# One attention half prepared earlier, weight splits ordered behind units, partial sums in score tiles, and chunk order 0, 2, 1

## The chip, the cores and the metric

The kernel runs on one core of one Trainium2 chip. The metric is the device time of one execution in microseconds (us). Engines are named as in the profile: PE (matmul), PEld (its weight loads), DVE (VectorE), ACT (ScalarE), POOL (GpSimd) and SP, whose queue issues nearly all DMAs.

## What is computed

Three stages follow each other. Inputs q, k, v and alpha are [4, 8, 768, 48] (batch, heads, steps, head size).

```python
for t in range(S):
    state = alpha[:, :, t, :, None] * state + einsum(k[:, :, t], v[:, :, t])
    y[:, :, t] = einsum(q[:, :, t], state)
x = y.transpose(0, 2, 1, 3).reshape(3072, 384)

h = x @ w_in                       # 384 -> 2048
g = (a0 + a1*h + a2*h**2 + a3*h**3) / (1 + |b0|*|h| + |b1|*h**2 + 1e-6)
x = g @ w_out                      # 2048 -> 384

h = x @ w2_in                      # 384 -> 1024
solu = h * softmax(h)
out = (layernorm(solu) * g_ln) @ w2_out
```

## The kernel before

Steps are cut into six chunks of 128 (times four batches: 512 tokens a chunk). Every product is computed with operands split into a high and a low part (three matmuls for one: hi*hi, hi*lo, lo*hi).

**First stage, by halves.** A chunk's attention is done in two halves of two batches, so there are 12 halves, numbered 0 to 11; the "fourth half" is index 3, the "fifth" index 4. `a_prep(i)` prepares a half: DVE transposes alpha, k and q (L294, L299), runs two scans over alpha (L312, L321), multiplies k by the second (L324) and transposes it back (L328); POOL multiplies q by the first (L339). The result goes to scratch memory (`kb_d`, `qk_d`) and is read back in another layout (`qks`, L280; `kns`, L286). `a_pe(i)` computes the half: scores (`sc`, L424), copied to tiles `A` by ACT (L431) and masked by POOL (L432), then `y` (L448), written as a high and a low part of the token tile `xt` (L474 on ACT, L475 on DVE), then the state update (`u`, L487). `qks`, `kns` and the scratch tiles of the preparation exist once.

**Second stage, by units.** A unit is one chunk and one block of 128 of the 2048 hidden columns; there are 96, numbered u = 0 to 95. `m_up(u)` is nine matmuls into one of three banks `h` (L604) and a chain of elementwise operations on ACT and DVE, with POOL in some units (L609 to L635); its last DVE operation, L628 or L635, is recorded as `fin[u]` and frees the bank. `gh` (ACT) and `gl` (POOL, L638) are the parts of the result. `m_down(u)` follows four units later: nine matmuls (L650) into three accumulation banks of the chunk. The order of units is written by hand: chunk 0 blocks 0 to 11 (u = 0 to 11), chunk 1 blocks 0 to 7 (u = 12 to 19), chunk 0 blocks 12 to 15, chunk 1 blocks 8 to 15, then chunks 2 to 5. So the sums of chunks 0 and 1 leave in two parts (`x2b_d` and `x2_d`; `x2e`, L657 to L660), which are added when the third stage loads them (`n_load`, L686 to L699).

**Weights.** Group n holds blocks 4n to 4n+3. `w1_group(n)` loads and splits it in seven steps (`split_w`: load to a staging tile `st` or a lent place, three DVE operations L541, L544 and L545, a copy on ACT and a difference on POOL). `w2_split` does the same for the third stage in 14 steps and writes the parts to scratch memory.

**Third stage.** Tiles of 128 tokens: `n_up`, softmax and norm, `n_turn`, `n_down`, `n_out`. The four tiles of the first chunk are put among the last units; the other tiles follow the last unit. `n_load` writes to the buffers of tag `xt`, of which there are two, so the second chunk's load waits for the last unit's up matmuls.

**What sets the order.** The loop over u (L895 on) calls, in this order: a weight step (`take(prep, 1)`; `CONV` says at which u a group begins), `m_up(u)`, a step of the half in work (`take(side, 1)`; `BEGIN` says at which u a half begins), a step of `w2_split` at u = 20, 31, 32, 39, 40 and so on, and `m_down(u - 4)`. A step of a half (`half_steps`) is one step of `a_pe(i)` and two of the preparation of half i+1; `LINGER = {3: 16}` makes the preparation of half 4 wait until u = 16, although half 3 begins at u = 8. The framework then orders each engine's instructions with a simulated timeline; the resulting queues are fixed. `tc.issue_after(x)` makes the instructions of a block on x's engine come behind x. `pin(n)` does that for a unit's last PE instruction at u and for ACT, POOL and `fin` at u - n; `later(n)` for `fin[u - n]` alone:

```python
def later(n):
    return tc.issue_after(fin[now[0] - n].ins) if n <= now[0] < GE + n and now[0] - n in fin else ExitStack()
```

Weight groups two and three are not pinned.

Of the kernel before, what the change touches and what calls it, by code (L numbers as in the profile page):

```python
# [30 lines left out]
def kernel(  # L31
# [21 lines left out]
    CH = 128  # L53
# [20 lines left out]
    PRE = (1, 1, 0, 0)  # L74
    GP = 2
    GS = 2
    G1 = 99
    G2 = 3
    MIX = lambda u: u < 24 and u % 2 == 0
    EARLY = (9, 11, 13, 15)  # L80
    SKIP = (5, 7, 11)
    AHEAD = 3
    U2, IDLE = 20, (0, NF1 // 2 - 1)
    BEGIN = {2: 2, 8: 3, 21: 4, 27: 5}
    BEGIN.update({16 * c + 2 + 8 * x: 2 * c + 2 + x for c in range(2, NCH - 1) for x in range(2)})
    CONV = {0: 2, 13: 3}
    LINGER = {3: 16}
    assert (B, H, D, CH) == (4, 8, 48, 128)

    const = ctx.enter_context(tc.tile_pool(name="const", bufs=1, side="left"))  # L90
# [66 lines left out]
    def network(fast):  # L157
# [257 lines left out]
        def a_pe(i):  # L415
# [4 lines left out]
            for p in range(2):  # L420
                sc = [ps_ap.tile([128, B, CH], F32, name="sc", tag="at") for j in range(2)]
                for x in range(B):
                    for j in range(2):
                        nc.tensor.matmul(  # L424
                            sc[j][:, x, :],
                            lhsT=hf.k[p][64 * j:64 * j + D, x, :], rhs=hf.q[p][64 * j:64 * j + D, x, :],
                            start=True, stop=True,
                        )
                for j in range(2):
                    t = A[p, j] = ap_.tile([128, B, CH], F32, name="A", tag=f"A{p}{j}")  # L430
                    nc.scalar.activation(t, sc[j], AF.Copy)  # L431
                    nc.gpsimd.affine_select(  # L432
                        out=t, in_=t, pattern=[[0, B], [1, CH]], compare_op=ALU.is_ge, fill=0.0, base=0,
                        channel_multiplier=-1,
                    )
                yield
# [204 lines left out]
        def m_down(u):  # L641
            c, f = order[u]
            n, o = divmod(f, 4)
            if (c, f) in first:
                x2ps[c] = [ps_x2p.tile([128, NTOK], F32, name=f"x2p{d}", tag=f"x2p{d}") for d in range(KT)]
            gh, gl = gts.pop(u)
            hi, lo = wo[n]
            for d in range(KT):
                for w, gg in ((hi, gh), (hi, gl), (lo, gh)):
                    nc.tensor.matmul(  # L650
                        x2ps[c][d], lhsT=w[:, o, 128 * d:128 * d + 128], rhs=gg,
                        start=((c, f) in first and w is hi and gg is gh), stop=((c, f) in final and w is lo),
                    )
            if (c, f) in final:
                to = x2_d[c] if f == NF1 - 1 else x2b_d[c]
                for d0, n in ((0, 2), (2, 1)):
                    e = moe_pool.tile([128, 2, NTOK], F32, name="x2e", tag="st", bufs=2)  # L657
                    for d in range(n):
                        nc.scalar.activation(e[:, d], x2ps[c][d0 + d], AF.Copy, scale=back if fast else 1.0)  # L659
                    nc.sync.dma_start(out=to[:, d0:d0 + n, :], in_=e[:, :n])  # L660
                del x2ps[c]
# [23 lines left out]

        def n_load(c):  # L686
            t = x2s[c] = moe_pool.tile([128, KT, 2, NTOK], F32R, name="x2", tag="xt", bufs=2)
            for kt in range(KT):
                raw = t[:, kt, 1].bitcast(F32)
                nc.sync.dma_start(out=raw, in_=x2_d[c][:, kt, :])  # L690
# [109 lines left out]

        def n_out(s, op):
            c, qq = divmod(s, 4)
            o = moe_pool.tile([128, DM], F32, name="o", tag="st", bufs=2)
            nc.scalar.activation(o, op, AF.Copy)
            to = out.rearrange("(b c q j) d -> c q b j d", b=B, c=NCH, q=4)[c, qq]
            for b in range(B):
                (nc.scalar if s == NCH * B - 1 and b >= 2 else nc.sync).dma_start(out=to[b], in_=o[32 * b:32 * b + 32])
# [64 lines left out]
        def half_steps(i):  # L872
            gp = a_pe(i)
            gd = chain(a_prep(i + 1), a_move_qk(i + 1) if i + 1 >= NPE else iter(()), a_load(i + 2, ("ra", "rk")) if i + 2 < NH and i + 1 >= NPE else iter(())) if i + 1 < NH else iter(())
            b = "wait"
            while True:
                with pin(GP):
                    a = next(gp, "end")
                if now[0] >= LINGER.get(i, 0):
                    with pin(GS):  # L880
                        b = next(gd, "end")
                        if b != "end":
                            b = next(gd, "end")
                if a == "end" and b == "end":
                    if i + 1 < NH:
                        _run(a_enter(i + 1))
                        if i + 2 < NH and i + 1 < NPE:
                            _run(a_load(i + 2))
                    return
                yield  # L890
# [5 lines left out]
        for u in range(NU + LAG):  # L896
# [5 lines left out]
            if u < NU:  # L902
# [7 lines left out]
                if fast and u in CONV:  # L910
                    _run(prep)
                    stage["near"] = CONV[u] == 2
                    prep = w1_group(CONV[u])
                take(prep, 1)
                m_up(u)
            if u == NU:
                _run(n_load(1))
            take(side, 1)
            if u == U2 or (u > U2 and u % (NF1 // 2) in IDLE and u not in (23, 24)):
                stage["bank"] = "at" if fast else ""  # L920
                with later(G2):
                    take(split2, 1)
# [150 lines left out]
```

## Time and profile before

| | us |
|---|---|
| median of 3 runs (794.39 to 795.79) | 794.52 |
| the profiled execution's own time | 793.51 |
| its span, first to last instruction | 791.8 |
| PE busy | 735.1 |
| DVE busy | 624.9 |
| ACT busy | 540.1 |
| POOL busy | 351.0 |

Shares of busy time are means over stages with different limits. Windows of the span, with the busy time of each engine in each, say more, and the timeline says at which instruction an engine stood and what released it. Units run from about 57 to 594 us, the third stage to the end.

### The profile page before, as it was taken

The page shows a single profiled execution, that of the slowest core. Times are in us where ns is not written, and L with a number is a line of the kernel's source. Part 1 is how long each engine was busy: PE and PEld are TensorE (multiplying, and loading weights), DVE is VectorE, ACT ScalarE, POOL GpSimd, SP SyncE. Part 2 cuts the span into 40 slices and gives each one's busy share as a digit, 9 for nine tenths or more (in the row PEclk, how much of TensorE's full clock was granted, in tenths as well). Part 3 has the DMA queues.
Part 4 walks back from the last instruction along what each step waited for, and adds up shares of the span by engine and source line. Part 5 has one row for each costly group of instructions (what it writes and reads, how often), then busy time and mean ns, then how long its engine had stood idle before and what let it go on. Part 6 is the DMA issues. An engine that isn't in the chain of part 4 may idle for free.

```text
span 791.8 us, 13947 instructions
## 1 busy us (share of the span) xinstructions
PE 735.1 (93%) x4976; PEld 612.2 (77%) x4976; DVE 624.9 (79%) x1116; ACT 540.1 (68%) x989; POOL 351.0 (44%) x306
## 2 busy tenths in 40 slices
PE   4783999977999999999999999999998999999996
PEld 4672788865778787877877788888876988898996
DVE  5999884888889998989898977677875878676730
ACT  2246676866787888788878898888864645645532
POOL 3266674755634454443544444342234433532322
PEclk9857899988999999999999999999999999999999
DMA  7986270246567476546735460840035152551443
GB/s 175 276 249 172 69 193 2 72 135 172 182 141 204 112 218 162 139 93 203 159 121 121 151 151 1 287 172 0 2 120 146 60 141 79 139 129 47 114 109 83
DMA packets 88719, 104.90 MB, mean 132 GB/s; under 512 B 34624, under 2 KB 63296, under 8 KB 88640
## 3 DMA queue, kind: packets, MB, share of 16 engines
q1 hardware_dynamic: 88544, 103.81, 48.6%
q8 instruction: 41, 0.67, 0.4%
q14 instruction: 38, 0.31, 0.1%
q10 hardware_dynamic: 96, 0.10, 0.0%
HBM read 62.17 MB, written 29.13 MB: 115 GB/s over the span
## 4 chain that ended last, share of the span: by engine, by line
PE 51%; DVE 23%; ACT 9%; DMA 7%; issue 5%; SPq 3%; POOL 2%; DVEq 0%; ACTq 0%; POOLq 0%
PE h L731 13%; PE op L795 12%; PE x2p L650 11%; PE hp L604 11%; DVE w L633 2%; PE y L448 2%; DVE p L630 2%; DVE hp L634 2%; DVE P L312 2%; PE sc L424 2%; DMA rq<-in_q_dram 2%; DVE fp L544 2%; DVE p L635 1%; SPq L270 1%; DVE fp L541 1%
## 5 line engine op out<-in xcount | busy, mean ns | idle before, releaser
L604 PE MATMUL hp<-xt,g 128*128 128x512 f32 x864 | 225.8, 403 | 9.5 <-DVE p L628 7.5
L638 POOL TENSOR_TENSOR gl<-p,gh 128x512 fp32r<-128x512 f32 x96 | 127.0, 1323 | 199.1 <-ACT gh L637 111.3
L604 PEld LDWEIGHTS hp<-xt,g 128*128 128x128 f32 x864 | 164.3, 193 | 49.4 <-DVE p L628 8.3
L650 PE MATMUL x2p<-gh,g 128*128 128x512 f32 x576 | 196.5, 397 | 1.4 <-ACT x2e L659 1.4
L650 PEld LDWEIGHTS x2p<-gh,g 128*128 128x128 f32 x576 | 108.9, 189 | 28.2 <-ACT x2e L659 3.5
L650 PE MATMUL x2p<-gl,g 128*128 128x512 f32 x288 | 114.1, 396 | 1.1 <-POOL gl L638 1.1
L795 PE MATMUL op<-w2oh,room 128*128 128x384 f32 x384 | 101.7, 339 | 0.2 <-DVE room L787 0.2
L731 PE MATMUL h<-w2ih,x 128*128 128x512 f32 x288 | 93.1, 399 | 3.0 <-ACT x L697 2.7
L787 POOL TENSOR_TENSOR room<-room,room 128x1024 fp32r<-128x1024 f32 x22 | 54.1, 2464 | 93.7 <-ACT room L786 93.6
L633 DVE SCALAR_TENSOR_TENSOR w<-w,co,hp 128x512 f32<-128x512 f32 x84 | 62.0, 738 | 41.1 <-ACT hp L632 40.4
L609 ACT ACTIVATE ah<-hp 128x512 f32<-128x512 f32 x96 | 56.9, 593 | 26.5 <-PE hp L604 25.5
L611 ACT ACTIVATE p<-hp,co 128x512 f32<-128x512 f32 x96 | 65.9, 687 | 8.3 <-POOL gl L638 8.1
L612 ACT ACTIVATE w<-ah,co 128x512 f32<-128x512 f32 x96 | 69.4, 724 | 2.8 <-DVE hp L634 2.4
L795 PEld LDWEIGHTS op<-w2oh,room 128*128 128x128 f32 x384 | 70.1, 188 | 1.4 <-DVE room L787 0.5
L630 DVE SCALAR_TENSOR_TENSOR p<-p,co,hp 128x512 f32<-128x512 f32 x84 | 61.9, 737 | 10.0 <-ACT p L611 9.6
L632 ACT ACTIVATE hp<-ah 128x512 f32<-128x512 f32 x84 | 50.3, 598 | 26.3 <-DVE p L630 25.3
L731 PEld LDWEIGHTS h<-w2ih,x 128*128 128x128 f32 x288 | 54.5, 190 | 15.7 <-ACT x L697 3.1
L650 PEld LDWEIGHTS x2p<-gl,g 128*128 128x128 f32 x288 | 54.6, 189 | 13.6 <-POOL gl L638 1.6
L795 PE MATMUL op<-w2ol,room 128*128 128x384 f32 x192 | 65.0, 339 | 0.0
L637 ACT ACTIVATE gh<-p 128x512 fp32r<-128x512 f32 x96 | 59.9, 625 | 6.8 <-PE x2p L650 4.2
L635 DVE SCALAR_TENSOR_TENSOR p<-p,co,hp 128x512 f32<-128x512 f32 x84 | 62.0, 739 | 1.2
L631 ACT ACTIVATE ah<-w,co 128x512 f32<-128x512 f32 x84 | 60.6, 721 | 1.1
(168 smaller groups left out, 1263.0 us busy)
## 6 DMA issues: line engine op xcount, KB each, us to landing
room<-room SPq DMA_DIRECT2D x96, 128.0 KB, 2.4
qk_d<-qk SPq DMA_DIRECT2D x10, 771.0 KB, 4.7
st<-in_moe_w_in_dram SPq DMA_DIRECT2D x13, 512.0 KB, 5.1
st<-in_moe_w_out_dram SPq DMA_DIRECT2D x16, 384.0 KB, 4.2
qks<-qk_d SPq DMA_DIRECT2D x20, 257.0 KB, 4.9
x<-x_d SPq DMA_DIRECT2D x18, 256.0 KB, 3.2
out_dram<-o SPq DMA_DIRECT2D x94, 48.0 KB, 1.6
ra<-in_alpha_dram SPq DMA_DIRECT2D x44, 96.0 KB, 2.7
```

The costliest lines, as they stand in the source:

```text
L604: last["PE", u] = nc.tensor.matmul(hp, lhsT=w[:, kt, 128 * o:128 * o + 128], rhs=xts[c][:, kt, xx, :], start=(kt == 0 and w is hi and xx = ...
L611: nc.scalar.activation(p, hp, AF.Square, bias=co[:, 7:8])
L612: nc.scalar.activation(w, ah, AF.Square, bias=co[:, 6:7])
L630: nc.vector.scalar_tensor_tensor(p, p, a1, hp, ALU.add, ALU.mult)
L631: nc.scalar.activation(ah, w, AF.Ln, bias=rest)
L633: nc.vector.scalar_tensor_tensor(w, w, rest, hp, ALU.add, ALU.mult)
L635: fin[u] = nc.vector.scalar_tensor_tensor(p, p, a0, hp, ALU.add, ALU.mult)
L637: last["ACT", u] = nc.scalar.activation(gh, p, AF.Copy)
L638: last["POOL", u] = nc.gpsimd.tensor_tensor(gl, p, gh[:].bitcast(F32), ALU.subtract)
L650: nc.tensor.matmul(x2ps[c][d], lhsT=w[:, o, 128 * d:128 * d + 128], rhs=gg, start=((c, f) in first and w is hi and gg is gh), stop=((c, f) ...
L731: nc.tensor.matmul(hp[:, 512 * n:512 * n + 512], lhsT=x2s[c][:, kt, x, CH * b:CH * b + CH], rhs=w2[w][:, kt, 512 * n:512 * n + 512], start ...
L795: nc.tensor.matmul(op, lhsT=x[:, 128 * f:128 * f + 128], rhs=w2[w][:, f, :], start=(f == 0 and x is hi and w == "oh"), stop=(f == NF2 - 1 ...
```

## The change

- `LINGER` goes: the fifth half's preparation runs with the steps of the fourth half, as for the others.
- The third and fourth half begin one unit later (u = 3 and 9), group two's split too (u = 1). The begins of the fifth and sixth are kept.
- The split steps of groups two and three are pinned behind the `fin` of the unit before (`later(G1)`, G1 = 1).
- The first step of `w2_split` moves from u = 20 to u = 33; the others keep their places.
- The two score tiles of a pair become one tile of two slots, with the same memory. The first partial sums (chunk 0, unit 11, done at u = 15) are copied to these tiles and not to staging tiles `st`.
- In the third stage chunk 2 is taken before chunk 1 (`TURN`).

```diff
--- before.py
+++ after.py
@@ -74,17 +74,17 @@
     PRE = (1, 1, 0, 0)
     GP = 2
     GS = 2
-    G1 = 99
+    G1 = 1
     G2 = 3
     MIX = lambda u: u < 24 and u % 2 == 0
     EARLY = (9, 11, 13, 15)
     SKIP = (5, 7, 11)
     AHEAD = 3
-    U2, IDLE = 20, (0, NF1 // 2 - 1)
-    BEGIN = {2: 2, 8: 3, 21: 4, 27: 5}
+    U2, IDLE = 2 * NF1 - 1, (0, NF1 // 2 - 1)
+    BEGIN = {3: 2, 9: 3, 21: 4, 27: 5}
     BEGIN.update({16 * c + 2 + 8 * x: 2 * c + 2 + x for c in range(2, NCH - 1) for x in range(2)})
-    CONV = {0: 2, 13: 3}
-    LINGER = {3: 16}
+    CONV = {1: 2, 13: 3}
+    TURN = (0, 2, 1) + tuple(range(3, NCH))
     assert (B, H, D, CH) == (4, 8, 48, 128)
 
     const = ctx.enter_context(tc.tile_pool(name="const", bufs=1, side="left"))
@@ -426,8 +426,9 @@
                             lhsT=hf.k[p][64 * j:64 * j + D, x, :], rhs=hf.q[p][64 * j:64 * j + D, x, :],
                             start=True, stop=True,
                         )
+                both = ap_.tile([128, 2, B, CH], F32, name="A", tag=f"A{p}")
                 for j in range(2):
-                    t = A[p, j] = ap_.tile([128, B, CH], F32, name="A", tag=f"A{p}{j}")
+                    t = A[p, j] = both[:, j]
                     nc.scalar.activation(t, sc[j], AF.Copy)
                     nc.gpsimd.affine_select(
                         out=t, in_=t, pattern=[[0, B], [1, CH]], compare_op=ALU.is_ge, fill=0.0, base=0,
@@ -654,7 +655,10 @@
             if (c, f) in final:
                 to = x2_d[c] if f == NF1 - 1 else x2b_d[c]
                 for d0, n in ((0, 2), (2, 1)):
-                    e = moe_pool.tile([128, 2, NTOK], F32, name="x2e", tag="st", bufs=2)
+                    if u == 11 and fast:
+                        e = ap_.tile([128, 2, NTOK], F32, name="x2e", tag=f"A{d0 // 2}")
+                    else:
+                        e = moe_pool.tile([128, 2, NTOK], F32, name="x2e", tag="st", bufs=2)
                     for d in range(n):
                         nc.scalar.activation(e[:, d], x2ps[c][d0 + d], AF.Copy, scale=back if fast else 1.0)
                     nc.sync.dma_start(out=to[:, d0:d0 + n, :], in_=e[:, :n])
@@ -685,6 +689,7 @@
 
         def n_load(c):
             t = x2s[c] = moe_pool.tile([128, KT, 2, NTOK], F32R, name="x2", tag="xt", bufs=2)
+            c = TURN[c]
             for kt in range(KT):
                 raw = t[:, kt, 1].bitcast(F32)
                 nc.sync.dma_start(out=raw, in_=x2_d[c][:, kt, :])
@@ -800,6 +805,7 @@
 
         def n_out(s, op):
             c, qq = divmod(s, 4)
+            c = TURN[c]
             o = moe_pool.tile([128, DM], F32, name="o", tag="st", bufs=2)
             nc.scalar.activation(o, op, AF.Copy)
             to = out.rearrange("(b c q j) d -> c q b j d", b=B, c=NCH, q=4)[c, qq]
@@ -872,15 +878,13 @@
         def half_steps(i):
             gp = a_pe(i)
             gd = chain(a_prep(i + 1), a_move_qk(i + 1) if i + 1 >= NPE else iter(()), a_load(i + 2, ("ra", "rk")) if i + 2 < NH and i + 1 >= NPE else iter(())) if i + 1 < NH else iter(())
-            b = "wait"
             while True:
                 with pin(GP):
                     a = next(gp, "end")
-                if now[0] >= LINGER.get(i, 0):
-                    with pin(GS):
+                with pin(GS):
+                    b = next(gd, "end")
+                    if b != "end":
                         b = next(gd, "end")
-                        if b != "end":
-                            b = next(gd, "end")
                 if a == "end" and b == "end":
                     if i + 1 < NH:
                         _run(a_enter(i + 1))
@@ -911,12 +915,13 @@
                     _run(prep)
                     stage["near"] = CONV[u] == 2
                     prep = w1_group(CONV[u])
-                take(prep, 1)
+                with later(G1):
+                    take(prep, 1)
                 m_up(u)
             if u == NU:
                 _run(n_load(1))
             take(side, 1)
-            if u == U2 or (u > U2 and u % (NF1 // 2) in IDLE and u not in (23, 24)):
+            if u >= U2 and (u % (NF1 // 2) in IDLE or u == U2 + 2):
                 stage["bank"] = "at" if fast else ""
                 with later(G2):
                     take(split2, 1)
```

## Rows read from the trace of the kernel before

**Rows 1.** The page's 40 slices: PE's busy tenths.
```profile
PE   4783999977999999999999999999998999999996
```

**Rows 2.** Windows: length, busy of PE, PEld, DVE, ACT, POOL, granted clock, DMA share.
```profile
83.70:117.00 33.30, 33.30 (x268) 26.39 (x268) 28.77 (x47) 25.22 (x47) 24.14 (x23) 0.95 0.55 141
117.00:151.00 34.00, 34.00 (x281) 27.52 (x280) 21.64 (x33) 24.94 (x44) 20.67 (x22) 1.00 0.12 29
151.00:173.10 22.10, 17.88 (x79) 14.46 (x78) 17.86 (x32) 17.33 (x33) 12.35 (x11) 0.98 0.42 125
173.10:187.50 14.40, 11.13 (x27) 8.46 (x28) 12.12 (x21) 7.82 (x13) 8.44 (x8) 0.62 0.43 137
187.50:210.00 22.50, 20.31 (x96) 16.05 (x95) 20.99 (x36) 17.81 (x33) 14.33 (x14) 0.88 0.56 152
...
262.00:590.00 328.00, 323.84 (x2272) 261.26 (x2271) 280.48 (x451) 271.49 (x490) 134.85 (x123) 1.00 0.46 130
```

**Rows 3.** Timeline of PE, first matmuls of units 18, 19 and 20 (idle before, releaser).
```profile
163.28 2.20 PE L604 MATMUL hp<-xt,g 128*128 128x512 f32 x9
...
173.12 4.21 PE L604 MATMUL hp<-xt,g 128*128 128x512 f32 x9 [4.24 <-DVE p L628]
...
183.51 7.08 PE L604 MATMUL hp<-xt,g 128*128 128x512 f32 x18 [3.25 <-DVE p L628]
```

**Rows 4.** Timeline, all engines, 183 to 200 us: a split operation on DVE and what follows.
```profile
188.79 0.69 DVE L541 TENSOR_SCALAR fp<-st 128x512 int32<-128x512 int32 x1 [3.57 <-DMA st<-in_moe_w_in_dram]
...
189.39 0.68 DVE L634 SCALAR_TENSOR_TENSOR hp<-w,hp 128x512 f32<-128x512 f32 x1
```

**Rows 5.** Windows around the stretches at half clock, columns as in rows 2.
```profile
172.20:179.10 6.90, 5.98 (x14) 4.72 (x15) 6.90 (x12) 3.77 (x6) 4.85 (x4) 0.51 0.29 73
182.50:189.30 6.80, 5.79 (x14) 4.54 (x15) 3.23 (x6) 4.01 (x8) 6.15 (x5) 0.50 0.87 267
199.50:203.00 3.50, 3.50 (x10) 2.63 (x10) 3.50 (x8) 3.09 (x7) 2.02 (x3) 0.51 0.45 102
598.90:602.30 3.40, 3.40 (x10) 2.66 (x9) 3.13 (x5) 0.63 (x1) 1.63 (x2) 0.50 0.00 0
```

**Rows 6.** Windows, operations on alT (DVE), rk (PE, PEld, DVE, POOL), rq (DVE).
```profile
0.00:791.80 791.80, 84.24 (x101) 0.96 0.49 132
...
0.00:791.80 791.80, 2.88 (x32) 2.53 (x32) 16.12 (x40) 0.11 (x1) 0.96 0.49 132
...
0.00:791.80 791.80, 18.43 (x40) 0.96 0.49 132
```

**Rows 7.** Start: timelines of PE and DVE; window of operations on st (DVE first).
```profile
79.59 4.13 PE L424 MATMUL sc<-qks 48*128 48x128 f32 x16 [12.18 <-DMA qks<-qk_d]
83.66 3.83 PE L604 MATMUL hp<-xt,g 128*128 128x512 f32 x9
...
75.82 0.68 DVE L628 SCALAR_TENSOR_TENSOR p<-w,hp 128x512 f32<-128x512 f32 x1
...
66.00:77.00 11.00, 2.07 (x3) 0.00 (x0) 0.00 (x0) 0.67 0.74 216
```

**Rows 8.** Timelines of ACT and DVE: the fourth half's copies to the token tile.
```profile
133.60 0.87 ACT L474 ACTIVATE xt<-y 128x512 fp32r<-128x512 f32 x2 [2.58 <-PE y L448]
...
134.23 1.02 DVE L475 TENSOR_TENSOR xt<-y,xt 128x512 fp32r<-128x512 f32 x2
```

**Rows 9.** Timeline of PE at the change to the third stage.
```profile
592.38 0.50 PE L650 MATMUL x2p<-gl,g 128*128 128x512 f32 x1 [1.11 <-POOL gl L638]
...
596.69 0.96 PE L731 MATMUL h<-w2ih,x 128*128 128x512 f32 x3 [2.65 <-ACT x L697]
```

**Rows 10.** Timelines of SP and ACT: second chunk's first load; chunk 2's loads and first copy.
```profile
578.04 0.32 SPq L690 DMA_DIRECT2D x<-x_d  x1
...
586.37 1.27 SPq L690 DMA_DIRECT2D x<-x_d  x3
...
589.09 0.63 ACT L697 ACTIVATE x<-x 128x512 fp32r<-128x512 f32 x1 [5.19 <-DMA x<-x_d]
```

## The prediction

> **What bounds the kernel now.** I read the page's slices first, then windows, then the timeline of the engine that ends each wait. The slices say that TensorE (PE) is at nine tenths or more nearly everywhere; besides the tail, the dips are in slices 1 to 4, 9 and 10 (158 to 198 us) and 31 [rows 1]. The windows put numbers on that [rows 2]: from 262 to 590 us, 323.84 of 328 us are busy, so the bulk of the units runs at PE's pace and whatever PE loses earlier is lost from the end. From 83.7 to 151 us PE is never idle, yet VectorE (DVE) has 12.4 us free between 117 and 151 (34.00 - 21.64). From 151 to 210 us PE is busy for 17.88 + 11.13 + 20.31 = 49.3 of 59 us: 9.7 us idle. That is the hole the change is about.
>
> Who makes it? The first matmuls of units 19 and 20 start at 173.12 and 183.51, after 4.24 and 3.25 us of waiting for L628 on DVE [rows 3]. L628 is the last operation of an earlier unit, which frees one of three score banks "h". DVE was not slow there but full of other work: the fifth half's preparation (held back to unit 16), group three's splits and the first split of the last stage's weights all come between the units' own operations. One row shows how this hurts: at 188.79 DVE has stood 3.57 us before a split whose load was late, and the next unit operation, L634, starts only behind it [rows 4].
>
> Each such stop costs twice. Of three stretches of 172.2 to 203 us the granted clock is 0.50 or 0.51, that is 1.2 instead of 2.4 GHz, each begun around idle time; nine matmuls take 4.21 us at 173.12 and 2.20 at 163.28 [rows 3, 5]. PE is busy there for 5.98 + 5.79 + 3.50 = 15.3 us, half of which, 7.6 us, would not be needed at full clock. The hole is worth 9.7 + 7.6 = 17.3 us.
>
> **The change part by part.** Sums are made against the profiled execution's own 793.5 us (span 791.8); the median of the runs, 794.5, is 1.0 above, which I add at the end.
>
> *Fifth half's preparation with the fourth half (middle).* Its DVE work, from the sums of ten halves: 8.4 us on alT, 1.6 from rk, 1.8 from rq, in all 11.9 us, and under 0.5 for two tiny ones: 12.3 us [rows 6]. It moves from units 16 to 20 into units 9 to 13. The window 117 to 151 is just units 9 to 14 (their pace 34/6 = 5.7 us) and has 12.4 us free: 21.64 + 12.3 = 33.9 of 34.0 us. It fits on paper and no better. Its DMAs move too (four rq loads, two scratch writes, four qks reads, eight loads for the sixth half) into a stretch with a DMA share of 0.12 against 0.42 now [rows 2]. The qks reads wait in SP's queue until the fourth half's y matmuls are done; the loads of group three queue behind them, and the splits come later by that. POOL gets its one product there, with 13.3 us free of 34.
>
> *Group three pinned, the last stage's first split moved from unit 20 to 33, first sums through score tiles.* These take work from before the units' operations between 151 and 200. DVE then has 17.86 + 12.12 = 30.0 us less 12.3 and less one split of 2.1 (the three operations of a step take 2.07 us [rows 7]) = 15.6 of 36.5 us, so those units can run at PE's pace. The sums' copies no longer take staging tiles, so the w_out loads behind them start without waiting for the sums to be written out; this is part of the same hole and counted there. The score tiles they take are idle from the fourth half's y (unit 11) to the fifth's scores (unit 21). Pairing the score tiles adds no instruction; if a pair is tracked as one, a second copy may wait for the first select, which the down matmuls hide; 0 to 0.6 us each without that cover. At unit 33 the moved split takes 2.1 us of a DVE that is busy 85% of its time (280.48 of 328); with PE covered by earlier units it costs between 0 and the 3.57 us above; I take 0.3.
>
> *Fourth half one unit later.* Its y now comes at unit 11, and unit 12 is the first that reads its result. The copies after y take 0.87 us on ACT and 1.02 on DVE [rows 8]; between them and unit 12's matmuls stands one group of nine down matmuls, about 2.2 us. Bounds 0 to 1.9 us, and more only if DVE puts preparation first; I take 0.7.
>
> So of 17.3 us in the middle, bounds are 0 (the crowd only moves) and 17.3. Full DVE in units 9 to 14 will cost something. In the 83.7 to 117 window it is busy for 28.77 of 33.30 with preparation and splits beside units and PE never stops, which is nearest to the new state: I leave 4.3 us of new stalls and the 0.7, and take 12.3.
>
> *Start: third half and group two one unit later, pinned.* Now PE waits 12.18 us at 79.59 for the qks reads, with unit 3's matmuls queued behind; those then take 3.83 us at half clock [rows 7]. The third half now begins at unit 3 and its scores are pinned behind that unit's last matmul, so these come first, inside the wait. They need unit 0's end, now at 76.50 us (75.82 + 0.68). Three split steps, 6.2 us of DVE at 2.07 each, stood among units 0 and 1 from 66 to 77 and go behind them, so that end comes earlier by up to 6.2 us. If it didn't, unit 3 would end at 80.3, 0.7 late: gain 3.1. If the clock also came up sooner, the 16 score matmuls would save up to 1.8. Against it, the 6.2 us land mostly between 83.7 and 117, where DVE has 4.5 us free [rows 2]: up to 1.7 us lost. Bounds 1.4 (3.1 - 1.7) to 5.6 (3.83 + 1.8); I take 3.0, near the row.
>
> *End: chunk 2 ahead of chunk 1.* PE stands 2.65 us for the copy of x made from two partial sums and 1.1 for gl [rows 9], and then runs 3.4 us at half clock, 1.7 lost [rows 5]. Chunk 2 needs three loads and no sums; today its loads go at 586.37, and the first copy starts at 589.09, 2.7 us later. The second chunk's loads go at 578.04, when the last unit's up matmuls have left the buffer [rows 10], so its three copies can be done before 590, and PE needs them at 594.0 (596.69 - 2.65 [rows 9]). Gain 2.65 + 1.7 = 4.4, with gl's wait up to 5.5 (POOL no longer has x work ahead of gl); none if the copies are queued late all the same. Chunk 1 then has until four tiles later. I take 4.5.
>
> Sum: 12.3 - 0.3 + 3.0 + 4.5 = 19.5; 793.5 - 19.5 = 774.0, and with 1.0 for the median **775.0 us**.
>
> **The rivals.**
> *The crowd only moves.* 33.9 of 34.0 us on DVE leaves no slack, operations wait for each other besides, and the three-bank limit then stops PE in units 9 to 14 as it did at 19 and 20. For it: the sum. Against it: 83.7 to 117, where PE never waited. Middle gain 0: 793.5 - 7.5 + 0.3 + 1.0 = 787.3. Chance 0.13.
>
> *A convoy on DVE (slower).* In units 9 to 16 the preparation waits for POOL or DMA results, splits are pinned behind units' ends, and the fourth half's copies stand behind both. Every late input at the head holds all that follows, as at 188.79. Units 18 to 20 ran at 9.8 and 10.4 us each (163.28, 173.12, 183.51 [rows 3]); a unit at 10.1 loses 4.4 against 5.7. All gains, with the whole hole gone, are 17.3 - 0.3 + 3.0 + 4.5 = 24.5 us, so it decides from six such units on; seven make 30.8 - 24.5 = 6.3 us slower, 800.8. Against it: before, only three units ran so, with more work on DVE. Chance 0.09. The Trainium skill ("PSUM — Partial Sum Buffer", section "Engine vs sequencer instructions") states that VectorE's queue is strictly first in, first out; by that rule a pin turns each late unit's end into idle DVE, since a ready split can't fill it. The trace agrees at 188.79, 3.57 us.
>
> *The change moves nothing at start and end.* The planner that orders the queues may still put the third half's scores or the x copies where they block. Then 793.5 - 12.0 + 1.0 = 782.5. Chance 0.07.
>
> **How the numbers follow.** The forecast's case, 767 to 783, has 0.68; a convoy of five to six units, which cancels the gains, 0.03. What a measurement here can tell from none is 0.2%, 1.6 us. Faster is 0.68 + 0.13 + 0.07 = 0.88, same 0.03, slower 0.09. Its low end takes nearly every bound at its best (17.3 + 5.6 + 5.5 = 28.4 gives 766.1); the high end reaches past the first rival to 790.
>
> **What would show it.** Right: DVE near full from 117 to 151 us with PE at ten tenths, no wait for L628 above 1 us and clock 1.00 between 151 and 203; unit 3's matmuls before the third half's scores; x copies from x_d alone before 594 less the shift. Wrong: waits of L604 for DVE before unit 16, a clock of 0.5 between 110 and 150, unit 12 waiting for xt, or a wait for x at the stage change of over 2 us.

## The result, and the profile after

The changed kernel takes 787.74 us (median of 5 runs, 786.62 to 788.99) against 794.52: the ratio is 0.9912, 95% interval [0.9886, 0.9939]. It is faster by about 6.8 us, 0.9%; forecast were 19.5 us. The profiled execution took 788.75 us with a span of 786.9 (791.8 before). Lines of the changed kernel are one higher than before from L430 on and four or five higher from L659 on: L604 is L605, L628 is L629, L786 is L791.

Where did the time go? I cut both spans at five matmuls that every run has: the first of units 0, 8 and 60 (nine records of L605 each), the first of tile 5 of the last stage (counted from 0; 18 records of L736 each) and the end of the last one.

| stretch, us | before | after | difference | forecast |
|---|---|---|---|---|
| launch to unit 0 | 56.6 | 58.3 | +1.7 | 0 |
| unit 0 to unit 8 (start) | 53.9 | 49.0 | -4.9 | -3.0 |
| unit 8 to unit 60 (middle) | 284.5 | 281.7 | -2.8 | -12.0 |
| unit 60 to tile 5 (end of the units) | 208.1 | 201.4 | -6.7 | -4.5 |
| tile 5 to the last matmul (tail) | 182.1 | 189.1 | +7.0 | 0 |
| last matmul to the end | 6.5 | 7.4 | +0.9 | 0 |

The first row is not the change's: up to there the runs below spread from 56.2 to 58.6, and two whose code is the kernel before's up to there take 57.9. Start and end won more than forecast. Two steps failed: the middle won 2.8 of 12.0, and the tail gave back all that the end had won.

The slices of the changed kernel (their part of the page, 40 equal slices) show dips in 1 to 4 and 8 only, where rows 1 had 9, 10 and 31 beside the first four; the granted clock now falls in the last two:

```profile
PE   4687999799999999999999999999999999999986
PEclk9857899999999999999999999999999999999988
```

The windows of the changed kernel (length, busy of PE, PEld, DVE, ACT, POOL, granted clock, DMA share, GB/s; the first four answer to rows 2):

```profile
83.70:117.00 33.30, 32.61 (x245) 26.28 (x244) 33.09 (x57) 24.69 (x46) 23.03 (x20) 0.95 0.29 88
117.00:151.00 34.00, 33.68 (x308) 26.62 (x306) 21.55 (x37) 19.57 (x38) 20.19 (x19) 1.00 0.73 179
151.00:173.10 22.10, 16.66 (x69) 13.54 (x66) 19.34 (x32) 19.86 (x35) 16.24 (x15) 0.85 0.38 98
173.10:210.00 36.90, 36.22 (x295) 29.21 (x294) 34.12 (x60) 32.29 (x62) 25.86 (x24) 1.00 0.33 106
590.00:610.00 20.00, 20.00 (x97) 17.45 (x96) 16.40 (x26) 10.78 (x18) 7.83 (x5) 1.00 0.69 183
745.00:770.00 25.00, 22.11 (x109) 21.12 (x108) 7.97 (x16) 10.23 (x16) 8.76 (x4) 0.86 0.50 117
```

The last of these windows in the kernel before, where PE hardly stopped there:

```profile
745.00:770.00 25.00, 24.83 (x135) 23.68 (x135) 12.65 (x26) 11.43 (x21) 5.00 (x3) 1.00 0.36 83
```

From 173.1 to 210 PE is whole again at clock 1.00: units 18 to 20's waits [rows 3] and the half clock behind them [rows 5] are gone. From 590 to 610, where it stood for x and gl [rows 9], nothing is idle. But 117 to 151, which was to fill DVE, has DVE at 21.55 us, no more than before [rows 2]. The stretch that is full is the one ahead of it, 83.7 to 117: 33.09 of 33.30 us, where it was 28.77. A new hole stands at 151 to 173.1 (5.4 us idle), and another near the end (2.9 us). PE's timeline has the waits themselves (start, length, what, idle before and its releaser), first at the start, where rows 7 had 12.18 us, then in the new holes:

```profile
76.59 4.21 PE L605 MATMUL hp<-xt,g 128*128 128x512 f32 x9 [4.80 <-DVE p L629]
...
143.79 6.29 PE L605 MATMUL hp<-xt,g 128*128 128x512 f32 x27
150.01 1.14 PE L488 MATMUL u<-vns,kns 128*64 128x48 f32 x32
156.58 4.21 PE L605 MATMUL hp<-xt,g 128*128 128x512 f32 x9 [5.44 <-DVE p L629]
...
759.29 0.69 PE L800 MATMUL op<-w2oh,room 128*128 128x384 f32 x1 [2.63 <-ACT room L791]
```

**The middle.** Unit 11's matmuls begin at 124.0 (129.3 before), those of unit 12 only at 143.79 (138.6 before). Unit 12 is the first to read the fourth half's tile, and its copies come 8.8 us later than in rows 8. In those 19.8 us PE lives on down matmuls, y and scores, so it hardly stops (once, 0.32 us); but DVE and ACT run dry (rows of ACT and DVE in the changed kernel):

```profile
142.41 0.87 ACT L475 ACTIVATE xt<-y 128x512 fp32r<-128x512 f32 x2 [4.50 <-PE y L449]
```

```profile
143.04 1.02 DVE L476 TENSOR_TENSOR xt<-y,xt 128x512 fp32r<-128x512 f32 x2 [5.86 <-ACT xt L475]
150.41 0.76 DVE L623 SCALAR_TENSOR_TENSOR hp<-p,co,hp 128x512 f32<-128x512 f32 x1 [6.35 <-ACT p L612]
```

With no chain under way, unit 15 must wait until unit 12's whole chain has run: 5.44 us, and 4.21 us for its nine matmuls at half clock.

**The tail.** At 637 us GpSimd does three hi/lo differences in a row (each makes the low part of an operand: the tile less its high part), and exactly beside them three softmax operations on single columns take 2.1 to 2.3 us each; the same three took 0.14 to 0.16 us one tile earlier. POOL and DVE of the changed kernel:

```profile
637.39 7.14 POOL L792 TENSOR_TENSOR room<-room,room 128x1024 fp32r<-128x1024 f32 x3 [19.05 <-ACT room L791]
```

```profile
630.85 0.14 DVE L771 TENSOR_TENSOR sm<-sm 128x1 f32<-128x1 f32 x1
632.17 0.15 DVE L772 SCALAR_TENSOR_TENSOR sm<-sm 128x1 f32<-128x1 f32 x1
632.36 0.16 DVE L773 SCALAR_TENSOR_TENSOR sm<-sm 128x1 f32<-128x1 f32 x1
...
637.67 2.14 DVE L771 TENSOR_TENSOR sm<-sm 128x1 f32<-128x1 f32 x1 [1.86 <-ACT sm L770]
639.85 2.33 DVE L772 SCALAR_TENSOR_TENSOR sm<-sm 128x1 f32<-128x1 f32 x1
642.21 2.33 DVE L773 SCALAR_TENSOR_TENSOR sm<-sm 128x1 f32<-128x1 f32 x1
644.58 0.81 DVE L774 TENSOR_SCALAR room<-room,sm 128x1024 f32<-128x1024 f32 x1
646.64 1.20 DVE L755 TENSOR_REDUCE sm<-h 128x1 f32<-128x1024 f32 x1
```

The chain is 6.3 us late from there; at 756.7 PE has no tile left, stands 2.63 us and then runs at half clock until 765.4. That GpSimd's differences are slow themselves does not explain it: behind the three GpSimd stands idle for 8.44 us (until 652.96). The Trainium skill ("SBUF — State Buffer", section "SBUF: two separate sides") states that VectorE and GpSimd share a port pair which one instruction locks for its whole length, among others a GpSimd operation that reads SBUF (the memory in which tiles like `sm` and `room` lie) against a VectorE operation with two SBUF inputs. The trace agrees: L771 to L773 have two inputs each, and 0.15 us became 2.1 to 2.3, about the length of one difference (7.14 / 3 = 2.38); L757 and L768, with one input each, keep 0.11 to 0.16 us beside GpSimd's operations as elsewhere.

### The profile page after: what moved, and what is told of

It reads as the page before. It is cut to its first block, busy times and chain, and to the rows that moved or that the text cites. A ratio compares the mean times of both kernels' runs of the same rounds, so it can differ in the third digit from the quotient of the medians.

```text
span 786.9 us, 13946 instructions
## 1 busy us (share of the span) xinstructions
PE 738.5 (94%) x4976; PEld 615.0 (78%) x4976; DVE 633.7 (81%) x1116; ACT 536.7 (68%) x989; POOL 354.7 (45%) x306
## 4 chain that ended last, share of the span: by engine, by line
PE 36%; DVE 28%; ACT 13%; DMA 8%; issue 6%; SPq 5%; POOL 3%; ACTq 0%; DVEq 0%; POOLq 0%
PE hp L605 14%; PE x2p L651 12%; SPq L786 3%; DVE room L776 3%; PE op L800 2%; DVE room L759 2%; DVE w L634 2%; PE y L449 2%; PE sc L424 2%; ACT jk L761 2%; DMA room<-room 2%; DVE hp L635 2%; DVE p L631 2%; PE h L736 2%; DVE sm L755 2%
## 5 line engine op out<-in xcount | busy, mean ns | idle before, releaser
L605 PE MATMUL hp<-xt,g 128*128 128x512 f32 x864 | 225.0, 404 | 14.0 <-DVE p L629 10.2
L639 POOL TENSOR_TENSOR gl<-p,gh 128x512 fp32r<-128x512 f32 x96 | 129.4, 1348 | 186.0 <-ACT gh L638 101.0
L605 PEld LDWEIGHTS hp<-xt,g 128*128 128x128 f32 x864 | 164.9, 194 | 53.0 <-DVE p L629 10.5
L800 PE MATMUL op<-w2oh,room 128*128 128x384 f32 x384 | 104.1, 345 | 3.7 <-ACT room L791 2.6
L736 PE MATMUL h<-w2ih,x 128*128 128x512 f32 x288 | 91.1, 394 | 0.0
L736 PEld LDWEIGHTS h<-w2ih,x 128*128 128x128 f32 x288 | 53.9, 188 | 11.7
```

Source lines behind the costliest of these rows:

```text
L605: last["PE", u] = nc.tensor.matmul(hp, lhsT=w[:, kt, 128 * o:128 * o + 128], rhs=xts[c][:, kt, xx, :], start=(kt == 0 and w is hi and xx = ...
L639: last["POOL", u] = nc.gpsimd.tensor_tensor(gl, p, gh[:].bitcast(F32), ALU.subtract)
L736: nc.tensor.matmul(hp[:, 512 * n:512 * n + 512], lhsT=x2s[c][:, kt, x, CH * b:CH * b + CH], rhs=w2[w][:, kt, 512 * n:512 * n + 512], start ...
L800: nc.tensor.matmul(op, lhsT=x[:, 128 * f:128 * f + 128], rhs=w2[w][:, f, :], start=(f == 0 and x is hi and w == "oh"), stop=(f == NF2 - 1 ...
```

## The experiments

Theories for the hole at 151 us: 'the gate' (unit 12 waits for the fourth half's tile because its y stands a unit later) and 'the crowd' (the fifth half's preparation fills VectorE); for the tail: 'the port' (GpSimd's differences hold up VectorE's small operations). Each kernel was timed beside the kernel before, and ratios are to that; the median of the kernel before went from 793.9 to 795.1 us between these sessions. Stretches and rows are of one profiled execution each.

**1. y at unit 10 again** (in the changed kernel)

```
-            take(side, 1)
+            take(side, 2 if u == 9 else 1)
```

> The changed kernel with one edit: the fourth half takes two of its steps at unit 9, so that its y stands at unit 10 again, before unit 11's token tile is needed by unit 12; all else (the fifth half's preparation beside it, pins, score tiles, chunk order) stays. Theory 'the gate': the loss left in the middle (5.44 us of idle TensorE at 151.15 and half clock until 161.2) comes from unit 12 waiting for the fourth half's tile, which was ready only at 143.8. It expects unit 12's matmuls to start some 4 to 6 us after unit 11's, no wait of L605 for DVE over 2 us between 143 and 165, clock 1.00 there, and 5 to 7 us off the changed kernel's time: about 781 to 783. Rival 'the crowd moved': DVE is too full in units 9 to 14 with the preparation; a wait of L605 for L629 stays somewhere between 120 and 170 whatever the unit of y, and the time stays at 786 to 789.

787.73 us, ratio 0.9918 [0.9900, 0.9936]: nothing won. Its copies of y still come at 143.06, unit 12 at 145.1, and 4.47 us of wait stand at 157. So the unit at which y is issued doesn't set its time; something earlier does. 'The gate' as I had put it falls, yet DVE, idle for 7.42 us ahead of its copy, isn't crowded there either.

**2. Three differences on VectorE** (in the changed kernel)

```
-    FASTS = (0, 20)
+    FASTS = (0, 4, 5, 6, 20)
```

`FASTS` lists the output tiles whose difference is made on VectorE.

> The changed kernel with the hi/lo differences of output tiles 4, 5 and 6 on VectorE instead of GpSimd (three operations L792, at 637 to 645 us in the changed kernel's trace). Theory 'the port': three [128x1] operations of the softmax chain (L771 to L773) took 2.1 to 2.3 us each instead of 0.16 just beside these three differences; that put the chain behind and TensorE ran out of tiles at 756.7 (2.63 us idle, then half clock to 765.4). It expects those small operations at 0.2 us, no wait of TensorE for L791 over 0.5 us behind 700, clock 1.00 to the end, and 3 to 6 us off: about 782 to 785. Rival 'chain too late anyway': the chain is behind because the score tiles come in a new rhythm after the chunk order changed; the three differences cost DVE 1.2 us each themselves, the gap near 757 stays, and the time stays at 786 to 790.

781.57 us, ratio 0.9844 [0.9822, 0.9867]: 'the port' holds. The tail takes 182.2 us (182.1 before), with clock 1.00 and 24.84 of 25 us busy; in that kernel's DVE rows the small operations are short beside the differences, which cost 1.2 us each:

```profile
634.31 1.23 DVE L792 TENSOR_TENSOR room<-room,room 128x1024 fp32r<-128x1024 f32 x1 [1.01 <-ACT room L791]
635.46 0.15 DVE L771 TENSOR_TENSOR sm<-sm 128x1 f32<-128x1 f32 x1
635.80 0.15 DVE L772 SCALAR_TENSOR_TENSOR sm<-sm 128x1 f32<-128x1 f32 x1
636.00 0.14 DVE L773 SCALAR_TENSOR_TENSOR sm<-sm 128x1 f32<-128x1 f32 x1
```

```profile
743.00:768.00 25.00, 24.84 (x140) 24.43 (x140) 3.79 (x6) 7.39 (x11) 7.61 (x4) 1.00 0.56 133
```

**3. Both edits**

> Both edits of the two runs above in the changed kernel: y at unit 10, and the three differences on VectorE. If the two losses are apart, their gains add: 8 to 13 us off, 775 to 780, about what was predicted for the change. If the tail's chain gives back whatever the middle wins (as the changed kernel's last 50 us gave back 6 us), it stands no more than 2 us below the better of the two.

782.35 us, ratio 0.9858 [0.9836, 0.9881]: no better than the second alone. From here on the base is experiment 2's kernel.

**4 to 6. The chunk order and the differences in the kernel before.** Chunk 2 ahead of chunk 1 alone (TURN, as in the diff of the change):

> The kernel before with one part of the change: chunk 2 ahead of chunk 1 in the last stage. Prediction's step: 4.5 us (2.65 us of wait for x, 1.1 for gl, half clock after it), so 790 with no wait for x at the stage change. Rival 'given back in the tail': the stage change is free of waits but the softmax chain becomes the bound near the end, with a wait of TensorE for the split (L786 here) and a low clock after 740, and the time is within 1.5 us of 794.5.

795.78 us, ratio 1.0014 [0.9994, 1.0034]: worth nothing alone. Unit 60 to tile 5 takes 201.4 us (208.1 before), so the end's gain of 6.7 is there, and the tail takes 188.2, so 6.1 are given back: the rival. Its POOL does three differences in a row at 645.84, and beside them DVE shows two of the small operations lengthened, and behind them L771, which works on a whole tile and took 0.81 us one tile earlier:

```profile
645.84 7.42 POOL L789 TENSOR_TENSOR room<-room,room 128x1024 fp32r<-128x1024 f32 x3 [19.31 <-ACT room L788]
```

```profile
646.12 2.15 DVE L768 TENSOR_TENSOR sm<-sm 128x1 f32<-128x1 f32 x1 [2.11 <-ACT sm L767]
648.50 2.26 DVE L770 SCALAR_TENSOR_TENSOR sm<-sm 128x1 f32<-128x1 f32 x1
650.79 3.02 DVE L771 TENSOR_SCALAR room<-room,sm 128x1024 f32<-128x1024 f32 x1
```

The same with FASTS of experiment 2:

> The kernel before with chunk 2 ahead of chunk 1 (which alone gave 795.8 us) and the differences of output tiles 4, 5 and 6 on VectorE. Theory 'the end's gain was real and was given back': with the tail freed the predicted 4.5 us show: no wait for x at the stage change, none over 0.5 us for the split behind 740, clock 1.00 there, 788 to 791. Rival 'the order of the chunks is worth nothing': 793 to 796 although the tail has no wait.

788.60 us, ratio 0.9925 [0.9900, 0.9950]: 5.6 us faster than before, with 201.4 and 182.3 us in the two stretches. And FASTS without the order of the chunks, the control:

> The kernel before with only the differences of output tiles 4, 5 and 6 on VectorE. Its tail had no wait of TensorE over 0.5 us and full clock, so if the three differences only cost where the softmax chain ends last, nothing is won here: 793.5 to 795.5. If they are worth 6 us in any order of the chunks: 787 to 790.

795.70 us, ratio 1.0013 [0.9994, 1.0032]: nothing. The three differences cost time only where the softmax chain ends last, and with the new order of the chunks it does.

**7 and 8. One part each, in the kernel before.** The halves one unit later (BEGIN 3 and 9), LINGER kept:

> The kernel before with one part of the change: third half begun at unit 3, fourth at unit 9 (y at unit 11), while the fifth half's preparation keeps waiting for unit 16. Theory 'gate alone': moving y one unit later is enough to leave unit 12 late; a wait of L604 for DVE of 4 to 6 us then stands near 150 to 157 besides the old ones at 173 and 183, and the middle loses 5 to 8 us, while the start wins about 5: 792 to 797. Theory 'gate and crowd together': without the preparation in units 9 to 13 y comes soon enough, no wait over 1.5 us at 145 to 160, and the start's gain shows: 788 to 791.

788.62 us, ratio 0.9917 [0.9895, 0.9940], 5.6 us faster than before. Its start takes 50.8 us, its middle 281.8; y's copy comes at 134.38 and unit 12 at 138.5, though y stands at unit 11. A wait of 3.00 us at 151 is left: between the two theories. And LINGER emptied, the halves as before:

> The kernel before with one part of the change: the fifth half's preparation from unit 9 on instead of 16, fourth half still begun at unit 8 (y at unit 10). Theory 'crowd': DVE is too full, unit chains and with them y come late, and a wait of L604 for L628 over 3 us stands somewhere between 125 and 165: 789 to 796. Theory 'gate alone': with y at unit 10 there is no such wait, and the waits of 4.24 and 3.25 us with their half clock are gone or smaller: 779 to 786.

787.76 us, ratio 0.9906 [0.9884, 0.9928], 6.4 us faster: the middle falls to 276.9 us (-7.6) with one wait of 1.43 at 154.9 and one of 3.36 at 181.8. 'The crowd' as put falls: 12.3 us of the fifth half's preparation went into units 9 to 13 at next to no cost.

**9. The fifth half's preparation behind y** (on experiment 2's kernel: LINGER = {3: 12})

> The changed kernel with the three differences on VectorE (781.6 us in the run above) and the fifth half's preparation begun at unit 12, behind the fourth half's y, instead of with the fourth half at unit 9. If the preparation crowds DVE ahead of y: y's last matmul ends before 138 instead of 142.3, the wait of 5.4 us near 154 is gone or under 2 us, clock 1.00 from 120 to 200, and 4 to 7 us off: 775 to 778. If y's place in the program is what holds it, the hole stays and so do 781 to 783. If the preparation only moves the crowd, waits for L629 come back at 160 to 200, 782 to 790.

786.50 us, ratio 0.9892 [0.9868, 0.9916], 5 slower than its base. The hole stays and a second one comes, so it isn't the fifth half's preparation that holds up y:

```profile
154.95 4.21 PE L606 MATMUL hp<-xt,g 128*128 128x512 f32 x9 [5.45 <-DVE p L630]
173.52 3.81 PE L606 MATMUL hp<-xt,g 128*128 128x512 f32 x9 [3.38 <-DVE p L637]
```

**10 and 11. Units in order** (on experiment 2's kernel). In the changed kernel's row at 143.79 the 27 matmuls of units 12 to 14 are mixed: the signals that a score is complete come at 149.17, 149.62 and 150.08 (in the kernel before at 141.29, 144.40 and 149.16).

```
-                m_up(u)
+                with tc.issue_after(last["PE", u - 1].ins) if u in (13, 14) else ExitStack():
+                    m_up(u)
```

> The changed kernel with the three differences on VectorE (781.6 us) and the matmuls of units 13 and 14 ordered behind all of units 12 and 13. In the changed kernel the 27 matmuls of units 12 to 14 stand mixed in the queue: the first of the three scores is complete only at 149.2, 5.4 us after its first matmul, and all three within 0.9 us. If that mixing makes part of the hole, the first score is complete about 2.3 us after its first matmul, the wait of 5.45 us shrinks to about 2 to 2.5, and 3 to 5 us go (with half clock): 777 to 779. If the wait is set by something else (VectorE's queue), nothing changes: 781 to 782.5.

777.56 us, ratio 0.9780 [0.9755, 0.9806]: 4.0 us, as that theory had it. DVE's first operation comes at 144.44, 3.5 us after unit 12's first matmul instead of 6.6; of 5.44 us 1.22 are left, with 2.31 a little later, and the clock stays at 1.00:

```profile
140.97 6.30 PE L605 MATMUL hp<-xt,g 128*128 128x512 f32 x27
149.56 2.34 PE L605 MATMUL hp<-xt,g 128*128 128x512 f32 x9 [1.22 <-DVE p L629]
156.41 1.89 PE L605 MATMUL hp<-xt,g 128*128 128x512 f32 x7 [2.31 <-DVE p L636]
```

The same for units 1 and 2 (u in (1, 2, 13, 14)):

> The same base (777.6 us) with the matmuls of units 1 and 2 ordered behind all of units 0 and 1 as well. At the start units 0 and 1 stand mixed (62 to 67.4 us): both scores are complete only at the end, and unit 3 then waits 4.9 us for unit 0's end, with half clock after it. If the mixing costs there what it cost at units 12 to 14 (4.0 us), unit 0's score is complete some 2.5 us (half clock: up to 4) earlier, the wait at 70 to 75 shrinks to about 2, and 2 to 4 us go: 773.5 to 775.5. If VectorE's own queue (third half's preparation, splits) sets unit 0's end, the wait stays at 4.5 to 5 and the time at 777 to 778.5.

A miss: 782.71 us, ratio 0.9851 [0.9815, 0.9888]. The wait at the start is 6.30 us, not 2. The start is 1.4 us shorter than its base's, but the fourth half's copies come at 144.4 (139.6 in the base), unit 12 at 145.1 (141.0), and the middle is 4.8 us longer; why y is later there is open.

**12. Both groups unpinned** (on experiment 10's kernel: G1 = 99, CONV = {0: 2, 13: 3})

> The kernel of the last run (changed kernel, three differences on VectorE, units 12 to 14 in order; 777.6 us) with one part of the change undone: group two's splits begin at unit 0 again and neither group is pinned behind a unit's end. Theory 'the pin pushed the start into the fourth half': group two's seven steps stand between 76 and 120 us beside the fourth half's preparation, so the third half's y came at about 110 to 112 instead of 104, the qks reads at 113 to 117 instead of 106, and the fourth half's y at 140 to 142 instead of 134. It expects those three back at about 104, 106 and 134 to 136 and unit 12 before 138, no wait of L605 over 1 us at 145 to 160; but unit 3 then waits longer at the start (8 us instead of 4.9): 776 to 780. Rival 'y is late for another cause' (scores in pairs, steps one unit later): the times of y stay within 2 us of the changed kernel's and the loss at the start comes on top: 780 to 783.

780.18 us, ratio 0.9821 [0.9791, 0.9851]. The times of y are those the theory named: the third half's copies at 103.2, the qks reads at 105.7, the fourth half's copies at 134.0, unit 12 at 137.7. So group two's pin had pushed them. The price stands elsewhere, behind the splits of group three:

```profile
157.03 7.01 PE L605 MATMUL hp<-xt,g 128*128 128x512 f32 x18 [9.69 <-DVE p L629]
```

**13. Group two early, group three pinned** (on experiment 10's kernel)

```
-    CONV = {1: 2, 13: 3}
+    CONV = {0: 2, 13: 3}
...
-                with later(G1):
+                with later(G1 if u > 12 else 99):
```

> The kernel with units 12 to 14 in order and the differences on VectorE (777.6 us), with group two's splits again from unit 0 and unpinned, group three's still pinned. Unpinning both gave y at 134 and unit 12 at 137.7 but a wait of 9.7 us at 157, which stood behind group three's splits, and 7.6 us at unit 3: 780.2. If that wait is group three's alone, it is gone or under 3 us here, the start's longer wait (2.7 us more) stays, unit 16 begins at 151 to 155 instead of 156.4, and the time is 773 to 777. If it comes from group two's place (units bunched behind an early y), the wait stays over 5 us and the time is 779 to 782.

772.98 us, ratio 0.9738 [0.9713, 0.9762], the fastest of all: 1.9% under the changed kernel, at the low end of what was expected. Against experiment 12 only group three's pin differs, 7.2 us; against experiment 10 only group two's place, 4.6 us (in the profiled executions 7.2 won in the middle, 2.4 lost at the start). From 151 to 210 PE is never idle:

```profile
66.00:117.00 51.00, 41.99 (x345) 33.63 (x345) 48.40 (x84) 41.22 (x75) 37.60 (x34) 0.93 0.62 158
117.00:151.00 34.00, 33.05 (x279) 26.48 (x278) 25.93 (x42) 24.82 (x47) 20.02 (x19) 1.00 0.48 125
151.00:210.00 59.00, 59.00 (x402) 47.49 (x401) 54.58 (x93) 52.93 (x96) 41.33 (x37) 1.00 0.47 126
```

How group two holds up y is seen on SP's queue. First the changed kernel, then this one (start, length, what): the preparation's kb write, the qk write and the qks reads all come 8 to 12 us later (2 of them by the later launch) where group two's seven steps stand beside the preparation instead of ahead of it. In the changed kernel the third half's copies (L475) come at 112.58, here at 102.57, and the next qks reads behind them: queue and ACT of the changed kernel, then of this one.

```profile
104.77 0.35 SPq L333 DMA_DIRECT2D kb_d<-alT  x1
...
110.19 0.39 SPq L341 DMA_DIRECT2D qk_d<-qk  x1
116.74 1.74 SPq L280 DMA_DIRECT2D qks<-qk_d  x4
...
112.58 0.87 ACT L475 ACTIVATE xt<-y 128x512 fp32r<-128x512 f32 x2 [1.97 <-PE y L449]
```

```profile
96.56 0.34 SPq L333 DMA_DIRECT2D kb_d<-alT  x1
...
100.57 0.39 SPq L341 DMA_DIRECT2D qk_d<-qk  x1
104.65 1.72 SPq L280 DMA_DIRECT2D qks<-qk_d  x4
...
102.57 0.85 ACT L475 ACTIVATE xt<-y 128x512 fp32r<-128x512 f32 x2
```

**14. Score pairs undone** (on experiment 10's kernel: four score tiles of their own, first sums through "st" tiles)

> The same base (777.6 us) with one part of the change undone: four score tiles of their own again, and the first sums leave through the staging tiles. Prediction's step: pairing costs 0 to 0.6 us a half where a second copy waits for the first select, the sums through score tiles spare the w_out loads of group three a wait. If the pairing delays the score copies and so y, the fourth half's y comes 2 us or more earlier (before 138) and up to 2 us are won; if the sums in the staging tiles hold up group three's loads, DVE stands for a load (DMA) around 155 to 170 and a wait for L629 or L636 over 2 us stands there: 779 to 784. If neither matters: 776.5 to 778.7.

782.36 us, ratio 0.9846 [0.9817, 0.9876], so this part is worth some 5 us here. y is no earlier (copies at 140.8), so the pairs cost nothing. The sums' writes go at 164.28 instead of 141.63 and the w_out loads behind them at 166.97 instead of 160.62; PE waits 4.53 us at 157.6 and 1.83 at 171.4.

**15. All differences on VectorE** (on experiment 10's kernel, `FASTS` with all 24 tiles)

> The kernel with units 12 to 14 in order (777.6 us), with every output tile's difference on VectorE, not only tiles 4, 5 and 6. Theory 'port only where it ends last': the small operations L771 to L773 lose more of their lengthening (their sum over the stage falls from 22 us by some 6 us), but VectorE gets 19 more operations of about 1.2 us in a stage that TensorE bounds; a gap opens only if VectorE stands for a late load: 776 to 780. If VectorE becomes the bound of the last stage, TensorE waits over 1 us for h or the split several times behind 610: 781 to 790.

778.74 us, ratio 0.9810 [0.9784, 0.9836], no gain and no loss beyond the intervals: the lengthening that is left in experiment 10's kernel costs nothing.

## Why the prediction was wrong

**Right.** The hole of 17.3 us was made of what was said: with units 18 to 20 rid of the crowd, waits and half clock at 173 to 203 us are gone, and 12.3 us of preparation fit into units 9 to 13 (experiment 8: 7.6 us of the middle by that part alone). The end was forecast at 4.5 us, at most 5.5; the stretch gained 6.7, in three different kernels alike (201.4 us in the changed kernel and in experiments 4 and 5). The waits of rows 9, a further 0.40 for x on POOL and the half clock make 5.9 of it; the rest is not explained. The start was forecast at 3.0 (bounds 1.4 to 5.6) and gained 4.9; unit 3's matmuls do come ahead of the third half's scores, and the wait there fell from 12.18 to 4.80 us. The size matches the prediction's 3.1 for an end of unit 0 that hardly moves (it comes at 76.53, before at 76.50; counted from unit 0's start 1.7 sooner) and its 1.8 for 16 score matmuls at full clock (2.3 us instead of 4.13).

**Wrong, first: that the 6.2 us of splits which land between 83.7 and 117 cost "up to 1.7 us", and with it that the fourth half one unit later costs "0 to 1.9 us".** Both were sized as busy time, and by busy time they hold: DVE is full there, 33.09 of 33.30 us, and PE hardly stops between 83.7 and 151 (66.3 of 67.3 us busy). What the pushed splits cost was the lateness of a chain that runs through this full DVE: third half's y at 112.6 instead of 102 to 105, its qks buffer free later, the fourth half's reads 10 us later, y's copy at 142.4 and unit 12 at 143.8. The price is paid behind it, when chains have run dry. From unit 0 to unit 12 the changed kernel takes 85.5 us, the kernel before 82.0: what the start wins never reaches the first unit that needs the fourth half. Experiment 13 against 10 puts 4.6 us on group two's place. The mixing of three units' matmuls, which the prediction had not looked for, puts 4.0 on top (experiment 10 against 2). By the ratios it is 3.3 and 5.1: the sum is firm, the share of each is not, to about a microsecond. With both taken away, unit 8 to unit 60 takes 271.9 us, 12.6 less than before, where 12.0 were forecast. So a middle of the forecast's size was there to be had, but only with an edit (units in order) that the change doesn't have; that the two numbers lie so close is in part luck. Of the signs of being wrong, two came true: "unit 12 waiting for xt", and waits for DVE before unit 16 (4.80 us at unit 3, 5.44 at unit 15). Of the signs of being right, "DVE near full from 117 to 151 us" did not (21.55 of 34).

**Wrong, second: the tail, for which nothing was forecast.** The sum took all gains through to the end, as if the last 180 us were PE's alone. They are so by little: with the chunks in a new order the softmax chain meets three of GpSimd's differences in a row, falls 6.3 us behind, and the end's gain comes back as a wait with half clock (experiments 2, 4, 5, 6). No term and no rival of the prediction stood for this.

**The sum, put right:** 6.8 us measured, 6.2 of the tail (787.7 to 781.6), 4.0 of the mixed units, 4.6 of group two make 21.5, or 773.0 us. These are steps from one median to the next, so they add up to experiment 13 by construction; that it lies near the forecast 775.0 is no proof of the forecast's sum. The rivals: the first, 'the crowd only moves', forecast 787.3, and 787.74 was measured, but by luck. DVE was not full from 117 to 151 and PE never waited for it between units 3 and 15; the rival has no gain in the middle, 7.5 us at start and end and nothing lost in the tail, where 2.8, 11.6 and 7.0 were measured. What is true in it is that the three-bank limit did stop PE, once, at unit 15, for a reason that it didn't name. No convoy formed; start and end moved.

## What to carry to other kernels

A step that is pushed behind others costs more than its engine time: follow the chain that it feeds (here splits, preparation, reads, y, token tile) to the first unit that needs its end, and ask at what time that end comes. A stage where the bound engine is 99% busy isn't safe: ask how late its feeder may be before it stops. And when several parts of a change pay less than their sum, undo one at a time on the best version so far: here group two's move undone, with two small edits beside it (three differences on VectorE, three units in order), made 773.0 of 787.7.

## What the runs showed that was not expected

Beside a difference of 128x1024 on GpSimd a one-column VectorE operation with two inputs took about as long as the difference: 2.14, 2.33 and 2.33 us instead of 0.15. Where such small operations form a serial chain, three of them cost 6.3 us, more than three such differences cost on VectorE (3 x 1.2 us). In experiment 4 a whole-tile operation was held up in the same way, 3.02 us instead of 0.81.

PE's clock after short stops: behind waits of 1.22 and 2.31 us the granted clock stayed at 1.00 (experiment 10), behind 2.63 us in the tail and 2.72 and 3.00 us in experiment 7 the matmuls that follow ran at 1.2 GHz (nine in 3.75 and 3.91 us instead of 2.2). The length of the stop alone doesn't tell: in experiment 1 a wait of 1.24 us at 262.8 was followed by 3.4 us at clock 0.50 (window below). Once it also fell with hardly a stop ahead of it: from 96.4 to 99.8 us the changed kernel's clock was 0.50, after score matmuls and one wait of 0.69 us (timeline of PE, then its window, then experiment 1's):

```profile
95.07 1.16 PE L424 MATMUL sc<-qks 48*128 48x128 f32 x8 [0.69 <-ACT A L432]
```

```profile
96.40:99.80 3.40, 3.40 (x9) 2.61 (x9) 3.40 (x6) 1.56 (x4) 3.29 (x3) 0.50 0.00 0
...
262.80:266.20 3.40, 3.39 (x8) 2.71 (x9) 3.40 (x6) 3.37 (x6) 0.35 (x1) 0.50 0.00 0
```
